# Linear attention and a gated feed-forward on one core: the order of batch 0's first steps, the pieces of w_out, and the last tile's banks

## The chip, the cores and the metric

The kernel runs on one core of one Trainium2 chip. The metric is the device time of an execution in microseconds (us). Before the change, four runs gave 313.59 to 313.95 us, with a median of 313.74 us.

A core has a matrix engine (TensorE, called PE in the profile), a vector engine (DVE), a scalar engine that evaluates functions (ACT), a general engine (POOL) and a synchronising engine (SP). Each has its own queue and runs it in order; they wait for one another through semaphores. POOL, SP and ACT also issue the transfers (DMAs) between main memory and on-chip memory. PE writes to PSUM, a small memory of eight banks of 512 float32 columns; DVE and ACT read results from there.

## The reference, cut to what matters

Eight batches of eight heads, 576 positions, head size 64. Linear attention comes first, then a gated feed-forward over all 4608 tokens of width 512 (inner width 1536):

```python
phi(x) = where(x > 0, x, exp(x) - 1) + 1
kv  = einsum('bhsd,bhse->bhde', phi(k), v)
z   = sum(phi(k), axis=positions)
num = einsum('bhsd,bhde->bhse', phi(q), kv)
den = einsum('bhsd,bhd->bhs', phi(q), z) + 1e-6
x   = (num / den), heads side by side          # 4608 x 512
g   = x @ w_gate
out = (silu(g) * (x @ w_val)) @ w_out
```

All inputs and the output are float32 in main memory; the kernel works in float16 with float32 sums.

## The kernel before, in words

**Tiling.** The 576 positions of a batch are cut into 9 slices (J) of 64. Two heads are stacked on the 128 partitions, so a tensor of one batch comes in two halves (lp = 0 and 1) of four heads each. The feed-forward works on groups of 512 tokens: eight units of 64 tokens each, nine groups in all. Group 0 is slices 0 to 7 of batch 0; group 1 takes slice 8 of batch 0 and slices 0 to 6 of batch 1. For a group, layer 1 has twelve steps (fb) of eight matmuls, 128x512 each, into a pair of PSUM banks; ACT takes the silu of the one bank, DVE multiplies by the other. Layer 2 has four tiles (t) of 128 tokens, with twelve matmuls each, whose result is copied to `osb` and stored in two DMAs.

**Order.** The order on each engine is the order in which the program's lines are written; nothing reorders it. PSUM is four pairs of banks (`pp4`), handed out in turn by `pair()`. Since phi(x) = max(x, 0) + min(exp(x), 1), phi of k is three steps: `exp_k` on ACT, `mx_k` and `mn_k` on DVE (and `add_k`, the sum of both).

**Batch 0's first steps** (the straight-line part from `nc.vector.tensor_copy(**q_cast(0))` on) are written by hand. q of batch 0 comes over SP. It is cast to float16, turned by PE into PSUM with 1 added (`q_one`, `q_turn`), two banks for each half: `qa` and `qb`. `q_exp` on ACT (L120) and `q_phi` on DVE (L454) make phi of q from each bank, four of each in all, written to `qT`. Meanwhile phi of k is made (L143, L147, L159). `zt` (L412) sums it over positions with small matmuls, and `zr_copy` (L416) brings the sums to `Zr`. `t_corners` (L254) multiplies `qT` by `Zr`, which gives the denominators. `lnrd` takes exp(-ln(den)) on ACT. `kv_corner` (L185) makes kv, `r_copy` (L201) brings it to `R`, `t_corners` with `R` gives the numerators, and `x_t` (L425) multiplies both into `xT`, the input of layer 1. `l1_mm` (L276) are the layer-1 matmuls of the first two steps, c being one of four slices of `xT`; later ones are at L292. `warm` issues matmuls (L124) whose result nobody reads.

The names X and Y are pairs made up of banks of `qb` and of another pair: Y's second bank is the one that holds the last quarter of turned q, so the second `t_corners(0, Zr, 1, Y)` can write it only when the last `q_phi` has read it.

**Loads.** POOL issues nearly all loads, in the written order; the program keeps eight of them on the way, so an issue waits until the one eight before it has landed. After the k and v of batch 0 and the layer-1 weights come, mixed: k of batch 1, w_out in pieces (`ld_w2`), q of batch 1 and its v. The twelve blocks of w_out are used by layer 2 of group 0 one after the other for all four tiles (L299). Inside that layer batch 1 is prepared: `s0` (after block 0) makes phi of q and k, `s1` (at block 6) turns q with 32 small matmuls (L374), `s2` (at block 7) sums z and turns slice 8, with copies at L381, L545 and L395, and after block 7 `s4` takes the denominators.

**The end.** The last tile of the last group is cut into columns 0 to 383 and 384 to 511 of one bank:

```python
for (n0, n1) in ((0, 384), (384, 512)):
    for fb in range(FB):
        l2_mm(g, t, fb, n0, n1)
    o = l2_out(g, t, "V" if n0 == 0 else "A", n0, n1, o)
```

`l2_out` copies with DVE ("V", L322) or ACT ("A", L120) and issues two stores (L326), on SP, but for the very last store, which ACT issues itself.

Of the kernel before, what the change touches and what calls it, by code (L numbers as in the profile page):

```python
# [17 lines left out]
def kernel(  # L18
# [10 lines left out]
    nc = tc.nc  # L29
# [9 lines left out]
    NG = B * J // U  # L39
# [22 lines left out]
    Zr = many([P, 2, 2, D], FP16, "Zr")  # L62
# [30 lines left out]
    def pair(p=None):  # L93
        i = 0 if p is None else [x is p for x in ring].index(True)
        p = ring.pop(i)
        ring.append(p)
        return p
# [4 lines left out]
    def ld(src, dst, b, lp):  # L102
        nc.gpsimd.dma_start(out=dst[b % NB][:, 2 * lp:2 * lp + 2, :],  # L103
                            in_=src[b].rearrange("(l a) (c j) d -> (a c) l (j d)", a=2, j=J)[:, 2 * lp:2 * lp + 2, :])
# [10 lines left out]
    def ld_w2(f0, f1):  # L115
        nc.gpsimd.dma_start(out=wo[:, f0:f1, :],
                            in_=moe_w_out[P * f0:P * f1, :].rearrange("(c p) f -> p c f", p=P))
# [4 lines left out]
    def warm(n, w=512, ps=None):  # L122
        for _ in range(n):
            nc.tensor.matmul(out=(ps or pp4[1][1])[:, 512 - w:512], lhsT=ones[:, :],  # L124
                             rhs=ones[:, 0:1].to_broadcast([P, w]), start=True, stop=True)
# [10 lines left out]
    def exp_k(b, lp):  # L136
        act(jl(ek, b, lp), lj(kr, b, lp), AF.Exp)
# [4 lines left out]
    def mx_k(b, lp):  # L142
        nc.vector.tensor_scalar(out=jl(kp, b, lp), in0=lj(kr, b, lp), scalar1=0.0, scalar2=None, op0=ALU.max)  # L143
# [35 lines left out]
    def kv_corner(b, lp, t, first, last):  # L179
        ps = kvp[b]  # L180
        for j in range(J):
            for l2 in range(2):
                for hh in range(2):
                    rows = slice(C * hh, C * hh + C)
                    nc.tensor.matmul(out=ps[hh][D * l2:D * l2 + D, D * lp:D * lp + D],  # L185
                                     lhsT=t[b % 2][rows, lp, j, D * l2:D * l2 + D],
                                     rhs=vr[b % NB][rows, 2 * lp + l2, D * j:D * j + D],
                                     start=(first and j == 0), stop=(last and j == J - 1))
# [107 lines left out]
    l2p = {}  # L296
# [17 lines left out]
    def l2_out(g, t, eng, n0=0, n1=512, o=None):  # L314
        if o is None:
            o = osb[on[0] % 4]
            on[0] += 1
        ps = l2p[(g, t)]
        if eng == "A":
            act(o[:, n0:n1], ps[:, n0:n1], scale=1.0 / SC)  # L320
        else:
            nc.vector.tensor_scalar(out=o[:, n0:n1], in0=ps[:, n0:n1], scalar1=1.0 / SC, scalar2=None, op0=ALU.mult)  # L322
        for e in range(2):
            b, j = units(g)[0][2 * t + e]
            dma = nc.scalar if g == NG - 1 and t == 3 and n1 == 512 and e == 1 else nc.sync
            dma.dma_start(out=out[S * b:S * b + S, n0:n1].rearrange("(c j) f -> j c f", j=J)[j],  # L326
                              in_=o[C * e:C * e + C, n0:n1])
        return o
# [17 lines left out]
    ld(k, kr, 1, 1)  # L346
    ld_w2(0, 4)
    ld(q, qr, 1, 0)
    ld(q, qr, 1, 1)
    ld_w2(4, 6)  # L350
    ld_w2(6, 8)
    ld_w2(8, 12)
    ld2(v, vr, 1)
# [56 lines left out]
    def zt(b, lp, ps, t, first, last):  # L410
        for j in range(J):
            nc.tensor.matmul(out=ps[:, 0:2], lhsT=t[b % 2][:, lp, j, :], rhs=ob[:, 0:P:C],  # L412
                             start=(first and j == 0), stop=(last and j == J - 1))

    def zr_copy(b, lp, ps):
        nc.vector.tensor_scalar(out=Zr[b][:, lp, :, :], in0=ps[:, 0:2].unsqueeze(2).to_broadcast([P, 2, D]),  # L416
                                scalar1=1.0 / SC, scalar2=None, op0=ALU.mult)

    def lnrd(ps, i, w0=0, w1=512):
        for l2 in range(2):  # L420
            act(lnt[2 * i + l2][:, w0:w1], ps[l2][:, w0:w1], AF.Ln, bias=epsb[:, 0:1])
            act(rd[i][:, l2, w0:w1], lnt[2 * i + l2][:, w0:w1], AF.Exp, scale=-1.0)
# [4 lines left out]
    def x_t(g, lp, ps, l2s=(0, 1)):  # L427
        for l2 in l2s:
            xmul(xT[g % 2][:, 2 * lp + l2, :], ps[l2][:, :], rd[lp][:, l2, :])

    def t_corners(g, W, lp, ps):
        for (b, j0, j1, c0) in units(g)[1]:
            corners(ps, W[b], b, lp, j0, j1, c0)
# [15 lines left out]
    def q_exp(lp, h, pair_):  # L449
        act(q_half(lp, h), pair_[h][:, :], AF.Exp, bias=m1[:, 0:1])  # L450

    def q_phi(lp, h, pair_):
        a = q_half(lp, h)
        nc.vector.scalar_tensor_tensor(out=a, in0=pair_[h][:, :], scalar=1.0, in1=a, op0=ALU.max, op1=ALU.min)  # L454

    kvp[0] = pp4[1]
    X = [pp4[0][0], pp4[3][0]]
# [17 lines left out]
    warm(WARM[1])  # L475
    q_turn(1, qb)
    q_exp(1, 0, qb)
    q_exp(1, 1, qb)
    exp_k(0, 0)
    warm(WARM[2])  # L480
    exp_k(0, 1)
    q_phi(0, 0, qa)
    q_phi(0, 1, qa)
    q_phi(1, 0, qb)
    mx_k(0, 0)
    q_phi(1, 1, qb)
    mn_k(0, 0)
    mx_k(0, 1)
    zt(0, 0, X[1], kp, True, False)
# [9 lines left out]
    kv_corner(0, 0, kp, True, True)  # L499
    r_copy(0, 0, 1, "VV")  # L500
    zt(0, 1, Y[0], ek, False, True)
    warm(WARM[5], ps=X[0])
    zr_copy(0, 1, Y[0])
    t_corners(0, R, 0, X)
    x_t(0, 0, X, (0,))
    kv_corner(0, 1, kp, True, False)
    kv_corner(0, 1, ek, False, True)
    r_copy(0, 1, 2, "VV")
    t_corners(0, Zr, 1, Y)
    lnrd(Y, 1)  # L510
    x_t(0, 0, X, (1,))
    l1_mm(0, 0, pp4[2], (0,))
    l1_mm(0, 1, X, (0,))
    t_corners(0, R, 1, pp4[1])
# [153 lines left out]
    for g in range(NG):  # L668
        b1, b2 = g + 1, g + 2
        if g == 0:  # L670
            sl = period0()
        else:
            sl, _ = none()
            late = []
            if g == 1:
                sl[1] = [lam(zsum, b1)]
                sl[4] = [lam(phi_q, b1, 0)]
                sl[5] = [lam(phi_q, b1, 1), lam(zb, b1)]
                ch = chain(b1, 6)
                late = ch.pop(10) + ch.pop(11)  # L680
            elif b1 < B:
                sl[0] = [lam(phi_q, b1, 0)]
                sl[1] = [lam(phi_q, b1, 1)]
                ch = chain(b1, 2)
            else:
                ch = {}
            for f, v_ in ch.items():
                sl[min(f, FB - 1)] += v_
        for fb in range(FB):
            if g == 0:  # L690
                if fb < 2:
                    continue
                if fb == 4:
                    ld2(k, kr, 2)
                    ld2(q, qr, 2)
                    ld2(v, vr, 2)
            if g == 1 and fb < 2:
                if fb == 0:
                    two = [pair(), pair()]
                    for cs in ((0, 1), (2, 3)):  # L700
                        for i in range(2):
                            l1_mm(g, i, two[i], cs)
                l1_post(g, fb, two[fb])
            else:
                l1(g, fb)
            for f in sl[fb]:
                f()
        if g + 3 < B:
            if g > 0:
                nc.gpsimd.tensor_copy(out=gate[:, :], in_=qT[b1 % 2][:, 1, J - 1, 1, C - 1:C])  # L710
            ld2(k, kr, g + 3)
            ld2(v, vr, g + 3)
            if g > 0:
                ld2(q, qr, g + 3)
        if g == 0:
            layer2_0()
            ld2(q, qr, 3)
        else:
            for f in late:
                f()  # L720
            for t in range(4):
                if t == 0 and b2 < B:
                    if g == 1:
                        nc.scalar.preload_act_table_set("natural_log_exp_and_others")
                    exp_k(b2, 0)
                    exp_k(b2, 1)
                    exp_q(b2, 0)
                    exp_q(b2, 1)
                    phi_k(b2, 0)
                    phi_k(b2, 1)  # L730
                    zsum(b2)
                if t == 1 and g == 1:
                    kv_all(b1)
                    r_copy(b1, 0, 2, "AA")
                if t == 3:
                    block(g)
                if g == NG - 1 and t == 3:
                    l2_open(g, t)
                    o = None
                    for (n0, n1) in ((0, 384), (384, 512)):  # L740
                        for fb in range(FB):
                            l2_mm(g, t, fb, n0, n1)
                        o = l2_out(g, t, "V" if n0 == 0 else "A", n0, n1, o)
                    continue
                lay2(g, t)
                l2_out(g, t, "A" if g == 1 and t == 1 else "AV"[t % 2])
            if b2 < B:
                zb(b2)
# [30 lines left out]
```

## Time and profile before

| What | Value |
|---|---|
| median of four runs | 313.74 us |
| the profiled execution's own time | 313.46 us |
| its span, first to last instruction | 311.7 us |
| PE busy | 304.8 us (98%) |
| DVE busy | 205.1 us (66%) |
| ACT busy | 152.6 us (49%) |
| layer-1 matmuls (L292) | 57.6% of the chain that ended last |
| layer-2 matmuls (L299) | 30.4% of that chain |
| read from main memory | 37.75 MB |

The profile is one execution. Its times count from the first instruction, and the time around the span (1.76 us here) is start and end of the execution. A row of the timeline gives start and length in us, engine, line and operation, what is written from what, the shape, how many, and in brackets the engine's idle time before it and what ended that. "The chain that ended last" is followed back from the last instruction, at each step to what released it. A transfer is shown with its issue; its landing is the issue plus the time to landing.

### The profile page before, as it was taken

Reading aid. Unit: us, or ns where it says so; the run is one execution under the profiler, and the core shown is the slowest. Engines: PE = TensorE matmul, PEld = TensorE weight load, DVE = VectorE, ACT = ScalarE, POOL = GpSimd, SP = SyncE. Lnnn points to the kernel's source line nnn. Section 1 sums busy time; section 2 is a strip of 40 time slices with the busy share of each in tenths; the row PEclk is TensorE's granted clock in tenths of the full one; section 3 lists DMA queues with packets and bytes.
Section 4 is the critical chain, followed back from the end, with each engine's and each line's share of the span. In section 5 each row is a group of like instructions: output and inputs, shape, how many; then the busy total and the mean of one; then the engine's idle time right before and its main releaser. Section 6 shows DMA issues by size and latency. Waiting matters only on the chain.

```text
span 311.7 us, 5565 instructions
## 1 busy us (share of the span) xinstructions
PE 304.8 (98%) x2206; PEld 141.7 (45%) x2206; DVE 205.1 (66%) x361; ACT 152.6 (49%) x231; POOL 48.5 (16%) x73
## 2 busy tenths in 40 slices
PE   7999999999999999999999999999999999999994
PEld 3444454444544454445444544454444444444442
DVE  4755868999699658976697759874981434143410
ACT  4865959448733844374536643574330333133311
POOL 8745444400000410041000500000000000000000
PEclk9999999999999999999999999999999999999999
DMA  8999999998502693239612990323032300140014
GB/s 218 198 197 200 206 207 236 234 207 147 118 13 39 98 196 110 40 57 184 162 38 41 130 235 12 64 52 87 0 75 53 85 1 1 43 93 0 2 34 101
DMA packets 41178, 32.80 MB, mean 105 GB/s; under 512 B 16448, under 2 KB 36160, under 8 KB 41152
## 3 DMA queue, kind: packets, MB, share of 16 engines
q0 software_dynamic: 20480, 18.29, 37.5%
q1 hardware_dynamic: 20592, 14.13, 18.9%
q8 instruction: 17, 0.28, 0.3%
q14 instruction: 9, 0.07, 0.1%
q10 hardware_dynamic: 80, 0.03, 0.0%
HBM read 37.75 MB, written 9.44 MB: 151 GB/s over the span
## 4 chain that ended last, share of the span: by engine, by line
PE 95%; DVE 2%; DMA 1%; SPq 0%; issue 0%; ACT 0%; DVEq 0%
PE pp L292 58%; PE pp L299 30%; PE pp L276 2%; PE pp L254 2%; PE pp L185 2%; DMA q<-in_q_dram 1%; DVE qT L454 1%; PE pp L124 1%; DVE xT L425 0%; PE pp L412 0%; PE pp L212 0%; PE pp L374 0%; DVE osb L322 0%; SPq L333 0%; DVE qp L467 0%
## 5 line engine op out<-in xcount | busy, mean ns | idle before, releaser
L120 ACT ACTIVATE sil<-pp 128x512 f16<-128x512 f32 x108 | 63.4, 597 | 101.0 <-PE pp L292 97.5
L292 PE MATMUL pp<-xT,wg 128*128 128x512 f16 x416 | 106.8, 379 | 0.0
L292 PE MATMUL pp<-xT,wv 128*128 128x512 f16 x416 | 106.8, 379 | 0.0
L285 DVE SCALAR_TENSOR_TENSOR hT<-pp,sil 128x512 f16<-128x512 f32 x108 | 72.3, 681 | 47.9 <-PE pp L292 35.3
L299 PE MATMUL pp<-wo,hT 128*128 128x512 f16 (+2 forms) x444 | 97.1, 373 | 0.6 <-DVE osb L322 0.6
L299 PEld LDWEIGHTS <-hT 128*128 128x128 f16 x444 | 41.9, 98 | 49.9 <-issue 2.1
L292 PEld LDWEIGHTS <-wv 128*128 128x128 f16 x416 | 40.7, 98 | 49.1
L292 PEld LDWEIGHTS <-wg 128*128 128x128 f16 x416 | 40.7, 98 | 48.4
L322 DVE TENSOR_SCALAR osb<-pp 128x512 f32<-128x512 f32 (+1 forms) x19 | 12.9, 682 | 31.1 <-PE pp L299 26.7
L120 ACT ACTIVATE osb<-pp 128x512 f32<-128x512 f32 (+1 forms) x18 | 10.3, 574 | 34.8 <-PE pp L299 34.8
L120 ACT ACT_TABLE_LOAD x13 | 16.7, 1283 | 2.5 <-PE pp L292 2.4
L120 ACT ACTIVATE ek<-kr 128x1152 f16<-128x1152 f16 x16 | 17.8, 1157 | 0.1
L229 DVE TENSOR_TENSOR qp<-qp,rden 128x1152 f16<-128x1152 f16 x12 | 16.2, 1346 | 0.0
L220 DVE TENSOR_REDUCE den<-prod 128x18 f32<-128x1152 f16 x12 | 16.1, 1344 | 0.0
L710 POOL COPY gate<-qT 128x1 f16<-128x1 f16 x4 | 1.1, 277 | 96.3 <-DMA qT<-qp 96.3
L120 ACT ACTIVATE eq<-qr 128x1152 f16<-128x1152 f16 x14 | 15.4, 1151 | 0.0
L103 POOL DMA_DIRECT2D vr<-in_v_dram x16 | 11.9, 744 | 8.5 <-DMA wo<-in_moe_w_out_dram 2.4
L271 DVE TENSOR_SCALAR xT<-pp 128x512 f16<-128x512 f32 (+1 forms) x14 | 8.8, 667 | 6.5 <-PE pp L254 6.5
L103 POOL DMA_DIRECT2D kr<-in_k_dram x16 | 11.6, 728 | 8.6 <-DMA wo<-in_moe_w_out_dram 1.9
L159 DVE TENSOR_TENSOR kp<-ek,kp 128x1152 f16<-128x1152 f16 x15 | 11.4, 758 | 0.5
L147 DVE TENSOR_SCALAR ek<-ek 128x1152 f16<-128x1152 f16 x16 | 7.8, 490 | 5.0 <-ACT ek L120 5.0
L103 POOL DMA_DIRECT2D qr<-in_q_dram x14 | 10.2, 729 | 5.3 <-DMA qr<-in_q_dram 2.3
(86 smaller groups left out, 179.5 us busy)
## 6 DMA issues: line engine op xcount, KB each, us to landing
out_dram<-osb SPq DMA_DIRECT2D x70, 128.0 KB, 2.8
kr<-in_k_dram POOLq DMA_DIRECT2D x16, 288.0 KB, 8.6
vr<-in_v_dram POOLq DMA_DIRECT2D x16, 288.0 KB, 10.1
qr<-in_q_dram POOLq DMA_DIRECT2D x14, 288.0 KB, 11.8
wg<-in_moe_w_gate_dram POOLq DMA_DIRECT2D x5, 256.0 KB, 9.4
wv<-in_moe_w_val_dram POOLq DMA_DIRECT2D x5, 256.0 KB, 10.3
q<-in_q_dram SPq DMA_DIRECT2D x2, 576.0 KB, 4.1
wo<-in_moe_w_out_dram POOLq DMA_DIRECT2D x2, 512.0 KB, 12.4
```

The costliest lines, as they stand in the source:

```text
L103: nc.gpsimd.dma_start(out=dst[b % NB][:, 2 * lp:2 * lp + 2, :], in_=src[b].rearrange("(l a) (c j) d -> (a c) l (j d)", a=2, j=J)[:, 2 * lp ...
L120: nc.scalar.activation(out=out, in_=in_, func=func, bias=bias, scale=scale)
L147: nc.vector.tensor_scalar(out=a, in0=a, scalar1=1.0, scalar2=None, op0=ALU.min)
L159: nc.vector.tensor_tensor(out=a, in0=ek[b % 2][:, lp, :, :], in1=a, op=ALU.add)
L185: nc.tensor.matmul(out=ps[hh][D * l2:D * l2 + D, D * lp:D * lp + D], lhsT=t[b % 2][rows, lp, j, D * l2:D * l2 + D], rhs=vr[b % NB][rows, 2 ...
L220: nc.vector.tensor_reduce(out=den[:, c, :], in_=prod[:, :, :].rearrange("p j (l d) -> p (j l) d", d=D), axis=AX.X, op=ALU.add)
L229: nc.vector.tensor_tensor(out=qv, in0=qv, in1=rden[:, c, :].unsqueeze(2).to_broadcast([P, 2 * J, D]), op=ALU.mult)
L271: nc.vector.tensor_scalar(out=dst, in0=ps[l2][:, c0:], scalar1=1.0 / SC, scalar2=None, op0=ALU.mult)
L285: nc.vector.scalar_tensor_tensor(out=hT[g % 2][:, fb, :], in0=ps[1][:, :], scalar=SC, in1=s[:, :], op0=ALU.mult, op1=ALU.mult)
L292: nc.tensor.matmul(out=ps[h][:, :], lhsT=w[:, c, P * fb:P * fb + P], rhs=xT[g % 2][:, c, :], start=(c == 0), stop=(c == 3))
L299: nc.tensor.matmul(out=l2p[(g, t)][:, n0:n1], lhsT=hT[g % 2][:, fb, P * t:P * t + P], rhs=wo[:, fb, n0:n1], start=(fb == 0), stop=(fb == F ...
L322: nc.vector.tensor_scalar(out=o[:, n0:n1], in0=ps[:, n0:n1], scalar1=1.0 / SC, scalar2=None, op0=ALU.mult)
```

## The change

There are four edits. In batch 0's first steps, ACT's first exp of k now stands ahead of q's last exp, DVE's first max of k ahead of q's third phi, and q's last phi behind the second z copy; the second denominators are taken before the second half of the kv matmuls of `ek`, and both first x products are issued together. One block of w_out is loaded between the two halves of batch 1's q, and the next one right behind them, in place of one piece of two blocks. The last tile is cut at column 320, its first part is copied by ACT and its second by DVE, the second part goes to the first bank of the next pair, and of each part's two stores ACT issues the second.

```diff
-            dma = nc.scalar if g == NG - 1 and t == 3 and n1 == 512 and e == 1 else nc.sync
+            dma = nc.scalar if g == NG - 1 and t == 3 and e == 1 else nc.sync
...
     ld(q, qr, 1, 0)
+    ld_w2(4, 5)
     ld(q, qr, 1, 1)
-    ld_w2(4, 6)
+    ld_w2(5, 6)
     ld_w2(6, 8)
...
     q_exp(1, 0, qb)
+    exp_k(0, 0)
     q_exp(1, 1, qb)
-    exp_k(0, 0)
     warm(WARM[2])
     exp_k(0, 1)
     q_phi(0, 0, qa)
     q_phi(0, 1, qa)
+    mx_k(0, 0)
     q_phi(1, 0, qb)
-    mx_k(0, 0)
-    q_phi(1, 1, qb)
     mn_k(0, 0)
     mx_k(0, 1)
...
     zt(0, 1, Y[0], ek, False, True)
+    zr_copy(0, 1, Y[0])
+    q_phi(1, 1, qb)
     warm(WARM[5], ps=X[0])
-    zr_copy(0, 1, Y[0])
     t_corners(0, R, 0, X)
-    x_t(0, 0, X, (0,))
+    x_t(0, 0, X)
     kv_corner(0, 1, kp, True, False)
+    t_corners(0, Zr, 1, Y)
+    lnrd(Y, 1)
     kv_corner(0, 1, ek, False, True)
     r_copy(0, 1, 2, "VV")
-    t_corners(0, Zr, 1, Y)
-    lnrd(Y, 1)
-    x_t(0, 0, X, (1,))
     l1_mm(0, 0, pp4[2], (0,))
...
-                    for (n0, n1) in ((0, 384), (384, 512)):
+                    for (n0, n1) in ((0, 320), (320, 512)):
                         for fb in range(FB):
                             l2_mm(g, t, fb, n0, n1)
-                        o = l2_out(g, t, "V" if n0 == 0 else "A", n0, n1, o)
+                        o = l2_out(g, t, "A" if n0 == 0 else "V", n0, n1, o)
+                        l2p[(g, t)] = pair()[0]
```

## The prediction

> **What bounds the kernel now.** I read the page first (TensorE, PE, is busy 98% of the span), then the chain of work that ended last in order of time, then the timeline of single engines where that chain leaves PE. The chain, as start and length in us:
>
> ```profile
> 8.64 0.38 DVE kp L143
> ...
> 9.06 0.39 PE pp L412 x9
> ...
> 14.76 0.38 PE pp L276
> 15.13 0.34 PE pp L254 x4
> 15.47 2.78 PE pp L276 x12
> 18.25 17.27 PE pp L292 x80
> ...
> 306.90 0.57 DVE osb L322
> ...
> 307.51 0.84 PE pp L299 x12
> ...
> 308.38 0.28 ACT osb L120
> ```
>
> From about 15.4 to 306.9 us PE is fed without a hole; that stretch is a fixed amount of matmul work that the change doesn't touch. So only three places can move the end: the head up to 15.4, the tail after 306.9, and a place in between where a transfer or the vector engine (DVE) is only just in time and a PE that comes earlier would have to wait. The head, by engine (start, length, what ended the idle time before it):
>
> ```profile
> 7.23 1.27 ACT L120 ACTIVATE qT<-pp,m 128x512 f16<-128x512 f32 x2 [0.41 <-PE pp L442]
> 8.38 1.16 ACT L120 ACTIVATE ek<-kr 128x1152 f16<-128x1152 f16 x1
> 8.55 0.45 DVE L143 TENSOR_SCALAR kp<-kr 128x1152 f16<-128x1152 f16 x1
> 8.92 0.68 DVE L454 SCALAR_TENSOR_TENSOR qT<-pp,qT 128x512 f16<-128x512 f32 x1
> 9.58 0.46 DVE L147 TENSOR_SCALAR ek<-ek 128x1152 f16<-128x1152 f16 x1
> 11.39 0.69 ACT L120 ACTIVATE lnt<-pp,epsb 128x512 f32<-128x512 f32 x1 [0.79 <-PE pp L254]
> ```
>
> The max of k (8.55) stands behind three phi steps of q, and ACT's first exp of k (8.38) behind four of q. The place in between is layer 2 of the first group, where batch 1's q arrives. POOL's queue tells the landings: each issue waits for the DMA eight issues before it, and its row names it.
>
> ```profile
> 34.47 0.71 POOL L103 DMA_DIRECT2D kr<-in_k_dram  x1 [1.90 <-DMA wo<-in_moe_w_out_dram]
> 35.88 0.80 POOL L103 DMA_DIRECT2D kr<-in_k_dram  x1 [0.70 <-DMA qr<-in_q_dram]
> 37.27 0.75 POOL L103 DMA_DIRECT2D qr<-in_q_dram  x1 [0.58 <-DMA qr<-in_q_dram]
> 38.55 0.71 POOL L103 DMA_DIRECT2D qr<-in_q_dram  x1 [0.53 <-DMA wo<-in_moe_w_out_dram]
> ```
>
> So w_out's first piece, q's two halves and w_out 4 to 6 are seen about 1.3 to 1.4 us apart. The second half of q was issued at 25.08 and took 11.9 us, so it landed at 36.98, and the vector engine picks it up a little later:
>
> ```profile
> 37.05 0.82 DVE L384 TENSOR_SCALAR qp<-qr 128x1152 f16<-128x1152 f16 x2
> 37.80 0.48 DVE L155 TENSOR_SCALAR eq<-eq 128x1152 f16<-128x1152 f16 x1
> ...
> 42.74 0.42 DVE L545 TENSOR_SCALAR Zr<-pp 128x256 f16<-128x256 f32 x1 [0.48 <-PE pp L543]
> 43.09 0.48 DVE L395 COPY qT<-pp 128x256 f16<-128x256 f16 x2
> ```
>
> PE's next num/den matmuls start at 43.62, right after the second copy ends (43.57). DVE works almost without a hole from 37.05; its only slack is the 0.48 us before 42.74.
>
> **Head: phi and exp moved.** No instruction is added or removed. ACT's first exp of k moves in front of q's last exp: from 8.38 to about 7.82 (7.23 plus half of the pair, 0.59); the k half has landed by then (POOL's issue at 7.59 was released by it). It ends at 8.98. On DVE the max of k takes the place of the third phi (7.95 instead of 8.55, ends 8.38 instead of 9.01), that phi follows, and the min can start at 9.01, when exp ends, instead of 9.58. On PE the two z sums with four warm-up matmuls between (0.86) start when the max ends: 8.43 instead of 9.06, and the second comes 0.63 earlier too, since the min (ends 9.47) and the warm-ups (end 9.52) are both done. From there the chain is z copy, denominator matmuls, and then eight ACT steps (ln, exp of the reciprocal) back to back from 11.39 to 16.45; all shift by 0.63. The last x product (16.49) and with it the last four layer-1 matmuls of the first pair shift likewise, and layer 1 starts at 17.46 instead of 18.09.
>
> What the moved work costs: q's last phi (0.68) now runs at about 12.02 to 12.70, behind the z copy. Waiting for it are the second denominator matmuls (13.41 before; now 12.75 at the soonest) and, queued behind it on DVE, the first x product: 13.10 before, now 12.63, only 0.47 earlier. Neither decides: ACT takes the second denominators only at 13.26, and the second x product waits for ACT's reciprocal at 13.33, 0.65 earlier than before. The kv copies of the second half now stand behind both x products, near 14.0 to 14.3 instead of 13.71 to 14.05, but the numerator matmuls that read them waited for the fourth layer-1 matmul (14.76), which waited for that x product; they still go out at 14.4 instead of 15.06. Sum of the head: PE is 0.63 earlier at layer 1. The weights allow it: w_val's second block is needed at 18.32 and lands at 18.0.
>
> **w_out in pieces around q.** The second half of q gets one 128 KB piece of w_out ahead of it. The pieces of 256 KB and the halves of 288 KB land 1.3 and 1.4 us apart, so 128 KB is 0.64. By the Trainium skill (DMA: Bandwidth & Descriptors, "Anatomy of one DMA — SWDGE (gpsimd) path") a DMA on this path costs about 2.0 us plus its bytes at 436 GB/s, which is 2.3 us for 128 KB. The first weight pieces speak for the smaller figure:
>
> ```profile
> wg<-in_moe_w_gate_dram POOLq DMA_DIRECT2D x2, 128.0 KB, 8.0
> wv<-in_moe_w_val_dram POOLq DMA_DIRECT2D x2, 128.0 KB, 7.9
> ```
>
> Issued at 4.30, 5.01, 5.72 and 6.48, they landed 8.0, 8.0, 7.9 and 7.9 us later, so 0.7 apart: in a full queue the fixed part overlaps. I take 0.64, with 0.5 and 2.3 as ends. POOL issues one DMA more (0.71), hidden in a queue that runs 11 to 12 us ahead of the landings; later loads carry the same bytes and land when they did.
>
> So q's second half lands at 37.62. DVE's second max of q starts at 37.64; queued behind it are all of q's and k's phi steps, the copies of the transposes and the two copies that release PE. Their chain in the trace, from the second max (37.42) to the end of the last copy (43.57), is 6.15 less the 0.48 of idle: 5.67. (The min at 37.80 waited for ACT's exp; that comes earlier now.) Start 37.64 gives 43.31, PE at 43.36 instead of 43.62. PE arrives at the transposes at 40.0 and waits about 0.6 there. Of the 0.63 that the head gains, 0.25 is left. The other w_out blocks come in time: block 4 is needed at 38.2 and is there at 36.3, block 5 at 39.0 and 38.3. Without this edit PE would wait about 0.15 for block 4 and q would be on time, so this edit by itself costs some 0.25.
>
> After 43.4 everything is 0.25 earlier. The next transfer with little slack is batch 1's v: its last half was issued at 31.86 and took 13.1, so it landed at 44.95, and is needed at 46.1 with the lead. The lead reaches the tail.
>
> **Tail.** Before, the last 128 columns wait until DVE has copied the first 384, because both are in one bank (PE's idle 0.65 is put down to "DVE osb L322"). Now the second part has a bank of its own that was last read in layer 1. PE runs all 12 x 512 columns without a hole: an ordinary tile takes 2.59, the tile before ended at 304.91, so PE is done at 307.50 instead of 308.35: 0.85. The last copy is 128x192 on DVE: from 0.56 for 384 and 0.69 for 512 columns, 0.36; the head's 128x128 at 0.29 says the same. It was 0.28 on ACT: minus 0.08. Handing over between engines, where ACT triggered its own DMA, minus 0.03. The last stores are 48 KB, between 32 KB (1.9 to 2.0) and 96 KB (2.1): minus 0.02. ACT's copy of 320 columns (0.44, between 0.28 and 0.60) and its first issue (0.56) end by 307.6, before the second issue at 307.9; SP likewise. Sum 0.72.
>
> **Sum.** 0.25 + 0.72 = 0.97 off the profiled execution's 313.46 (span 311.7, and 1.76 around it that nothing here touches): 312.5. That execution is 0.28 under the median of 313.74, so the median comes to 312.8.
>
> **Rivals.** (a) The lead of the head survives whole, if the piece delays q less or the chain behind it has more slack than I see: 0.63 + 0.72, 312.4. For it: DVE's short steps here take 0.45 to 0.64 for one size, so the chain has some give. Against it: the rows place q's landing only 0.44 before its use at 37.42, less than the piece's 0.64.
> (b) The lead is lost whole: q comes 0.9 or more later, or DVE's k phi steps are slowed by POOL's descriptor writing as at 40.23 (0.64, against 0.46 at 9.58). Only the tail is left: 313.0.
> (c) The tail doesn't pay: the second bank waits for something, or the stores end as late as before. Then 0.25 is left: 313.5.
> (d) Slower: the piece in front of q costs the page's 2.3. PE starts at 42.72 plus the piece, so above 0.90 the head loses, above 1.62 it eats the tail's gain and above 2.25 the kernel is slower by 0.2%. At 2.3 it is 1.40 lost and 0.72 gained: 314.4.
>
> **How the numbers follow.** Likeliest 0.57, (a) 0.16, (b) 0.13, (c) 0.08, (d) 0.06. A measurement of this kernel can tell about 0.2% (0.63 us) from no change. Likeliest and (a) lie beyond it, and (b) partly (0.03): faster 0.76; same 0.18 with (c) and most of (b); slower 0.06. The range from 312.3 to 313.3 holds the likeliest, (a) and (b).
>
> **What would show it.** Right: max of k near 7.9, the ln steps near 10.8, layer 1 at 17.5; a hole on PE before the transposes near 40.3, the denominators at 43.4; no hole between the last two parts and a last copy ending near 307.65 (307.90 less the 0.25). Wrong: a wait for q's second half well past 37.7, a wait for weights in layer 1 before 18.3, or a PE hole before the last 192 columns.

## The result, and the profile after

The changed kernel takes 312.78 us (median of 29 runs, 312.36 to 314.11); the kernel before, beside it, 313.60 (47 runs, 313.43 to 314.51). The ratio is 0.9974, with a 95% interval of 0.9969 to 0.9979: 0.26% less, or 0.82 us. The forecast was 312.8. The profiled execution took 312.39 (span 310.6), near the lowest of its runs, against 313.46 (span 311.7) before: 1.07 less. That the median shows less than the two profiles is something the forecast has no word for.

The chain of the work that ended last, of the changed kernel, through the head (start and length in us, what):

```profile
7.92 1.06 ACT ek L120
...
9.00 0.46 DVE ek L147
9.46 0.64 DVE kp L143
...
10.96 0.62 DVE ek L147
...
11.63 0.40 PE pp L413 x9
...
12.06 0.29 DVE Zr L417
12.35 0.61 DVE qT L455
...
13.00 0.40 PE pp L254 x2
...
13.74 0.97 PE pp L276 x4
14.71 0.34 PE pp L254 x4
15.05 2.78 PE pp L276 x12
17.83 17.27 PE pp L292 x80
```

The last row but one started at 15.47 before, and layer 1's steady run (last row) at 18.25: the head brought 0.42 us. Q's moved phi (12.35) stands on this chain, where the forecast had put it beside the chain. In the timeline layer 1's first matmul starts at 17.66 instead of 18.09, so I call the lead 0.43.

The second place, where batch 1's q arrives, on DVE (timeline of the changed kernel; the brackets say what ended the idle time):

```profile
36.63 0.45 DVE L385 TENSOR_SCALAR qp<-qr 128x1152 f16<-128x1152 f16 x1
37.58 0.46 DVE L385 TENSOR_SCALAR qp<-qr 128x1152 f16<-128x1152 f16 x1 [0.50 <-DMA qr<-in_q_dram]
37.96 0.45 DVE L155 TENSOR_SCALAR eq<-eq 128x1152 f16<-128x1152 f16 x1
...
42.32 0.42 DVE L545 TENSOR_SCALAR Zr<-pp 128x256 f16<-128x256 f32 x1
42.66 0.48 DVE L396 COPY qT<-pp 128x256 f16<-128x256 f16 x2
```

The two maxima that were one run at 37.05 are apart: the second waits 0.50 us for q's second half. The 0.48 us of idle before the copy to `Zr` is gone. The copies end at 43.14, and PE takes the denominators at 43.19 instead of 43.62: all of the 0.43 is still there.

The end (chain of the changed kernel):

```profile
296.72 10.40 PE pp L299 x60
307.12 0.02 issue
307.15 0.36 DVE osb L322
```

PE's last 60 matmuls are one piece; before, 48 and 12 with 0.65 between. The last copy ends at 307.51 instead of 308.66.

### The profile page after: what moved, and what is told of

Its sections match the earlier page's. It is cut to its first block, busy times and chain, and to the rows that moved or that the text cites. A ratio compares the mean times of both kernels' runs of the same rounds, so it can differ in the third digit from the quotient of the medians.

```text
span 310.6 us, 5568 instructions
## 1 busy us (share of the span) xinstructions
PE 304.4 (98%) x2206; PEld 141.9 (46%) x2206; DVE 204.7 (66%) x361; ACT 153.0 (49%) x231; POOL 48.8 (16%) x74
## 4 chain that ended last, share of the span: by engine, by line
PE 95%; DVE 1%; DMA 1%; ACT 1%; SPq 0%; issue 0%
PE pp L292 58%; PE pp L299 30%; PE pp L276 2%; PE pp L254 2%; PE pp L185 2%; DMA q<-in_q_dram 1%; DVE ek L147 0%; ACT ek L120 0%; ACT qT L120 0%; DVE kp L159 0%; PE pp L212 0%; DVE kp L143 0%; DVE qT L455 0%; PE pp L375 0%; DVE Zr L417 0%; SPq L333 0%
```

## The experiments

The first four kernels take the change apart. All four ran on one chip, beside the same runs of the kernel before (median 313.67).

**The tail alone.** The edit is the last part of the change's diff and its first line, on the kernel before.

```diff
-                    for (n0, n1) in ((0, 384), (384, 512)):
+                    for (n0, n1) in ((0, 320), (320, 512)):
...
-                        o = l2_out(g, t, "V" if n0 == 0 else "A", n0, n1, o)
+                        o = l2_out(g, t, "A" if n0 == 0 else "V", n0, n1, o)
+                        l2p[(g, t)] = pair()[0]
```

> The kernel before with the tail's edits alone (cut at 320, a bank of its own for the second part, ACT then DVE, ACT issues two stores). The forecast's sum: 0.72 us less than before. Read from the changed kernel's trace, where the last store took 2.12 us and not 2.0: 0.62 less. Rival (the tail doesn't pay): no change. PE without a hole ahead of the last 192 columns in all cases but the rival.

Measured: 313.03 us (11 runs, 312.73 to 313.25), ratio 0.9976 [0.9962, 0.9989], 0.64 less. This is most of the whole gain, and its runs lie within 0.5 us.

**The order of the first steps alone.** The diff's part from `q_exp(1, 0, qb)` to `l1_mm(0, 0, pp4[2], (0,))`.

> The kernel before with the order of batch 0's first steps alone. The forecast's lead is 0.63 us at layer 1, less about 0.15 of waiting for block 4 of w_out: 0.45 to 0.5 less than before. From the changed kernel's trace the lead is 0.43 only, since two of DVE's short steps take 0.25 longer, and block 4 is then just in time: 0.4 less. Rival (the lead is lost at the next transfer): under 0.1 less.

Measured: 313.43 us, but from 313.07 to 314.25 (11 runs), ratio 1.0001 [0.9991, 1.0010]. No sure gain: six runs lie 0.2 to 0.6 under the median of before, five at it or above. The profiled run (313.74) shows what the upper ones can look like (timeline of the order alone):

```profile
7.58 0.67 DVE L454 SCALAR_TENSOR_TENSOR qT<-pp,qT 128x512 f16<-128x512 f32 x1
...
8.71 1.16 ACT L120 ACTIVATE ek<-kr 128x1152 f16<-128x1152 f16 x1 [0.47 <-DMA kr<-in_k_dram]
8.71 0.46 DVE L143 TENSOR_SCALAR kp<-kr 128x1152 f16<-128x1152 f16 x1 [0.45 <-DMA kr<-in_k_dram]
```

K of batch 0 landed at 8.69, and both engines waited for it, 0.45 to 0.47 us; in the profile of before it had landed at 7.30. The old order wants k at 8.38, the new one at 7.82. Batch 0's q was late too: it landed at 6.19, in the profile of before at 5.89, and put these steps back by 0.3 us before k did. Layer 1 started at 18.34, later than the 18.09 of before.

**The pieces of w_out alone.**

```diff
+    ld_w2(4, 5)
     ld(q, qr, 1, 1)
-    ld_w2(4, 6)
+    ld_w2(5, 6)
```

> The kernel before with the pieces of w_out around q alone. q's second half lands 0.64 us later. The forecast's chain on DVE has 0.48 of idle to take that up, and q waited 0.44 before: no change in time, within 0.1. If a piece costs the page's 2.3 us: 1.4 slower.

Measured: 313.74 us (313.49 to 313.96), ratio 1.0003 [0.9994, 1.0012]: no difference. Q's second half landed 1.43 us after the piece, and the piece 0.61 after q's first half, so a piece in a full queue costs its bytes. The rival with 2.3 us is out. This trace also shows the old order with a late q of batch 0: it landed at 6.24, 0.35 later than in the profile of before, k (7.65) was in time, the max of k began at 8.89 and layer 1 at 18.43, both 0.34 later. So in the old order a late q went into the start of layer 1 in full.

**Order and tail, without the pieces.**

> The changed kernel without the pieces of w_out: order and tail alone. The forecast said that the pieces cost 0.25 us, so this one is 0.25 faster than the changed kernel, 1.2 less than before. The rival reading of the changed trace, in which PE had no wait for q at all at the transposes: the pieces cost nothing, and this is within 0.1 of the changed kernel, or slower by the wait for block 4 of w_out.

Measured: 312.72 us (312.30 to 313.45), ratio 0.9963 [0.9940, 0.9987]. The changed kernel has 312.78, so the pieces cost nothing that can be seen in the medians; these intervals are too wide to rule out 0.25, and the traces have to decide. In this one PE starts layer 2 at 34.86, reaches block 4 at 38.48 instead of 38.31 (16 matmuls of 0.216 us), because that block lands at 38.44, and takes the denominators at 43.29. Without the pieces PE waits 0.17 for w_out. With them q comes later, but in the first profile of the changed kernel the denominators followed layer 2's start by the same 8.26 us as before: nothing was lost. So the forecast's 0.25 for the pieces is wrong for these traces.

Beside the tail alone (313.03, on the same chip) this kernel shows what the order adds: 0.31 off the median, and nine of its eleven runs lie under 313.03. The intervals of the two ratios overlap, so the size of this is not sure.

**Q later still.** If q's landing is the next bound, a larger piece ahead of it must show at once.

```diff
-    ld_w2(4, 5)
+    ld_w2(4, 6)
     ld(q, qr, 1, 1)
-    ld_w2(5, 6)
```

> The changed kernel with blocks 4 and 5 of w_out in one piece ahead of the second half of batch 1's q, which so lands another 0.64 us later. If q's landing and DVE's chain behind it are the next bound, as the forecast has it, the denominators start 5.6 us after q lands: 0.65 us slower than the changed kernel, about 0.2 less than before. If that chain still has slack, no slower than the changed kernel.

Measured: 313.49 us (312.90 to 314.19, 10 runs), ratio 0.9995 [0.9986, 1.0003]: 0.7 slower than the changed kernel, as the bound has it. (The changed kernel's 312.78 was not taken beside this run; the kernel before has 313.58 beside this one and 313.60 beside that.) PE in that trace (timeline):

```profile
40.13 0.41 PE L374 MATMUL pp<-id,qp 64*128 64x64 f16 x16
41.01 0.41 PE L374 MATMUL pp<-id,qp 64*128 64x64 f16 x16 [0.48 <-DVE qp L387]
...
43.77 0.64 PE L254 MATMUL pp<-qT,Zr 64*64 64x64 f16 x16
```

The transposes are cut in two: the second half waits 0.48 us for DVE's sum of the second half of q. The wait that I had forecast for the changed kernel is here. Five traces side by side:

| Trace | q's second half lands | layer 2 starts | denominators start | after q | after layer 2's start |
|---|---|---|---|---|---|
| before | 36.98 | 35.36 | 43.62 | 6.64 | 8.26 |
| order and tail | 37.17 | 34.86 | 43.29 | 6.12 | 8.43 |
| changed | 37.56 | 34.93 | 43.19 | 5.63 | 8.26 |
| q later still | 38.15 | 34.85 | 43.77 | 5.62 | 8.92 |
| changed, second profile | 38.37 | 35.24 | 43.98 | 5.61 | 8.74 |

The denominators start 8.26 us after layer 2 begins or 5.62 after q lands, whichever is later; order and tail adds its 0.17 of waiting for block 4. With that, all thirteen traces fit to about 0.01. In the first profile of the changed kernel both are met at once, to within 0.01.

**One bank.** The tail's edits without the second bank.

```diff
-                        l2p[(g, t)] = pair()[0]
```

> The tail's edits alone, but both parts in one bank. If the second bank is what pays, PE waits for ACT's copy of 320 columns (0.44) and there is no gain: within 0.1 of before. If the other cut, the other engines and ACT's second store pay, most of the 0.64 of the tail stays.

Measured: 313.79 us (313.55 to 314.55), ratio 1.0005 [0.9996, 1.0015]. The whole gain of the tail hangs on this line (timeline of the kernel with one bank):

```profile
306.70 0.44 ACT L120 ACTIVATE osb<-pp 128x320 f32<-128x320 f32 x1 [1.03 <-PE pp L299]
...
307.19 1.15 PE L299 MATMUL pp<-wo,hT 128*128 128x192 f16 x12 [0.53 <-ACT osb L120]
...
308.44 0.36 DVE L322 TENSOR_SCALAR osb<-pp 128x192 f32<-128x192 f32 x1 [5.26 <-PE pp L299]
```

PE waits 0.53 us for ACT's copy. The other cut, the other engines and ACT's second store bring nothing without the second bank. The second bank with the old cut was not run.

**K later.** Whether k's landing bounds the new order, tried the other way: the first half of v goes ahead of k.

```diff
-    ld2(k, kr, 0)
-    ld2(v, vr, 0)
+    ld(v, vr, 0, 0)
+    ld2(k, kr, 0)
+    ld(v, vr, 0, 1)
```

> The changed kernel with the first half of batch 0's v loaded ahead of k, so that k lands 1.4 us later, near 8.8 to 9.5. If k's landing bounds the new order (in the trace of the order alone it landed at 8.69 and the max started at 8.71), the max of k waits for it and the head is 0.9 to 1.4 us later: 0.1 to 0.6 slower than before in spite of the tail. If k's landing doesn't bound it, as the forecast took it, no slower than the changed kernel.

Measured: 313.91 us (313.10 to 316.14, 10 runs), ratio 1.0010 [0.9993, 1.0027]: 1.1 slower than the changed kernel. K landed at 9.05 (timeline):

```profile
9.07 0.46 DVE L143 TENSOR_SCALAR kp<-kr 128x1152 f16<-128x1152 f16 x1 [1.16 <-DMA kr<-in_k_dram]
```

Against the changed kernel's profile the max of k starts 1.22 later, and layer 1 and the denominators 1.04 later. So a late k goes into the time nearly one to one. Where k is first and all of q comes over SP, nine traces put its landing at 7.20, 7.30, 7.39, 7.65, 7.91, 7.94, 8.02, 8.04 and 8.69. One of nine is past the 8.38 that the old order wants, five past the 7.82 of the new one, four of these by 0.22 at most.

**The changed kernel again**, with its own trace:

> The changed kernel itself, beside the next two on one chip: 0.8 us less than before as on record, with a spread of over 1 us.

Measured: 312.69 us (5 runs, 312.49 to 313.21; before 313.65 on this chip), ratio 0.9966 [0.9954, 0.9979]. The profiled run is the slowest of the five, and shows where else the lead goes (timeline of PE):

```profile
17.55 1.03 PE L292 MATMUL pp<-xT,wg 128*128 128x512 f16 x4
18.83 1.04 PE L292 MATMUL pp<-xT,wv 128*128 128x512 f16 x4 [0.25 <-DMA wv<-in_moe_w_val_dram]
```

Here the head's lead was 0.54. W_val's second block landed at 18.78 and not at 18.0, so PE waited for it (four matmuls take 0.86, the next four came 1.28 later), and q landed 0.8 later than in the first profile (last row of the table).

**Two tries to bring k sooner failed.** First, slice 8 of batch 0's q, needed only in layer 1, was loaded later on POOL's queue:

```diff
-        nc.sync.dma_start(out=q32[:, h:h + 2, :],
-                          in_=q[0].rearrange("(l a) (c j) d -> (a c) l (j d)", a=2, j=J)[:, h:h + 2, :])
+        nc.sync.dma_start(out=q32[:, h:h + 2, 0:8 * D],
+                          in_=q[0].rearrange("(l a) (c j) d -> (a c) l (j d)", a=2, j=J)[:, h:h + 2, 0:8 * D])
...
     ld_w1(512, 768)
+    nc.gpsimd.dma_start(out=q32[:, :, 8 * D:9 * D],
+                        in_=q[0].rearrange("(l a) (c j) d -> (a c) l (j d)", a=2, j=J)[:, :, 8 * D:9 * D])
```

> The changed kernel with slice 8 of batch 0's q, which is needed only in layer 1, loaded later on POOL's queue: 128 KB less ahead of k. q lands 0.3 and k 0.6 us earlier, so that k is there before the max wants it. If the landings at the start bound the head, it is 0.3 to 0.6 faster than the changed kernel, 1.1 to 1.4 less than before, with a smaller spread. If not, as fast as the changed kernel.

Measured: 313.13 us (312.74 to 314.13), ratio 0.9984 [0.9975, 0.9993]: by the medians 0.35 slower than the changed kernel, though the two intervals just touch; faster it is not. Q landed sooner (5.53), but in the profiled run, the slowest of twelve, k landed at 8.83. Second, the second half of q went to the head of POOL's queue:

```diff
-    for h in (0, 2):
-        nc.sync.dma_start(out=q32[:, h:h + 2, :],
+    for (h, dma) in ((0, nc.sync), (2, nc.gpsimd)):
+        dma.dma_start(out=q32[:, h:h + 2, :],
```

> The changed kernel with the second half of batch 0's q loaded at the head of POOL's queue and not on SP's, so that k follows q in one queue. In the traces so far k landed 1.3 to 3.3 us after q, which came over another queue, and 7.2 to 8.8 us from the start. If the late landings come from the two queues taking turns, k lands at 7.3 to 7.5 each time, the max of k starts at 7.9, and the time is that of the changed kernel's best executions: 1.0 to 1.1 less than before, with a spread of about 0.5. If k lands as late as before or q later than 5.9, no gain over the changed kernel.

> The order of batch 0's first steps alone, with the same load of q. Alone, without that load, the order gave no sure gain (ratio 1.000). If k's late landing had eaten it, 0.4 us less than before here. If the order has no gain of its own, none.

Measured: 314.73 us (ratio 1.0034 [1.0016, 1.0052]) and 316.79 us (1.0093 [1.0079, 1.0107]). This q landed at 7.50 and 7.33 instead of 5.9 and k behind it at 8.95 and 9.38, so neither run says anything on the order with an early k: the load that was moved came later itself. Why k's landing spreads is open: the next loads follow it at fixed steps of about 1.43 us, so it is the beginning of POOL's transfers that moves, but no run moved it on purpose without moving something else.

## Why the prediction was right, step by step

**Head, 0.63 forecast, 0.43 measured in the profile.** The first steps came as worked out: max at 7.85 (forecast 7.9), min at 9.00, second z sum at 9.52, ln at 10.80 (10.8). Then two durations failed. I took DVE's second max and second min of k as 0.45 us from the trace of before; they took 0.73 and 0.69 (timeline of the changed kernel):

```profile
9.11 0.74 POOL L112 DMA_DIRECT2D wv<-in_moe_w_val_dram  x1 [0.51 <-DMA kr<-in_k_dram]
9.38 0.73 DVE L143 TENSOR_SCALAR kp<-kr 128x1152 f16<-128x1152 f16 x1
...
10.58 0.74 POOL L112 DMA_DIRECT2D wg<-in_moe_w_gate_dram  x1 [0.73 <-DMA vr<-in_v_dram]
...
10.89 0.69 DVE L147 TENSOR_SCALAR ek<-ek 128x1152 f16<-128x1152 f16 x1
```

Both began inside an issue of POOL and ended 0.26 us after it. POOL's issues are tied to landings and hardly moved (9.01 and 10.49 before); DVE's steps moved under them. The long min held up the z sums, these the moved phi, that the second denominators, at 13.00 and not 12.75, and ACT took up its third ln at 13.44 instead of 13.26. So "Neither decides" was wrong: second denominators that come 0.25 late make the ln 0.18 late, so they had only 0.07 us to spare. Where the two steps were not stretched and k came at 7.94 or 7.91, the lead at layer 1 was 0.50 and 0.54. There ACT's first exp of k began when k was there, at 7.96 and 7.93 and not at 7.82; with that 0.14 and 0.11 the forecast's 0.63 is back. The chain was right, and two of its inputs, the length of DVE's steps and k's landing, were not. The old order meets POOL's issues too: in the traces of the tail alone and of one bank the second min took 0.72 us, and layer 1 began at 18.30 and 18.27; with the late q of the pieces alone it began at 18.43. The 18.09 that the lead is counted from is the earliest of these four.

**Pieces.** The piece's 0.64 was right (q at 37.56, forecast 37.62), and so was the chain behind q, to 0.11: from landing to denominators 5.63 against 5.74. That the edit costs 0.25 was wrong. It rested on a lead of 0.63; with 0.43 q's chain ends just when PE gets there anyway (with 0.5 some 0.07 would be lost), and without the pieces PE waits 0.17 for block 4. The forecast left 0.25 of the head; the profile kept 0.43. A lead that was sized too high and a loss that followed from it cancelled in part.

**Tail, 0.72 forecast, 0.62 in the profile, 0.64 in the median.** From the start of the last layer 2 to the end of the last copy the tail became 0.73 shorter (forecast 0.74). The last store took 2.12 us and not 2.02. But its size isn't the reason: in three other traces with the old tail ACT's last store, of 32 KB, took 2.12 to 2.13 as well. It was the trace of before that had a quick one, 2.03, and the forecast was built on it.

**Sum.** 0.97 forecast, 1.07 between the two profiles, 0.82 between the medians. That the forecast's 312.8 is met to 0.02 is luck: it took 313.74 from four runs as the median of before, where 47 runs give 313.60, and the gain is 0.15 smaller than forecast; the two errors cancel. That the medians show less than the profiles goes with the spread of the landings. The kernel before could wait for k until 8.38 and for q with 0.44 to spare; its runs lie close together. The new order has used these margins up, and an execution in which k, w_val or either q lands late gives part of the lead back. The runs with k and q later show the price, nearly one to one; how many ordinary runs pay it is argued from nine traces, not counted.

**Rivals.** (a), the lead survives, was right in the first profile's place (nothing was lost at q) and wrong on its size. (b), the lead is lost, is what single executions do, by late loads; its second reason, DVE's steps slowed beside POOL's issues, took 0.2 of the lead in the head. (c) is refuted by the tail alone, (d) by the pieces alone.

## What to carry to other kernels

When an engine is to start earlier, look for what it will then arrive at: here every 0.1 us beyond 0.43 would have met a landing, so the steady part of the gain was the bank at the end, and the order added about 0.3 us in most runs and nothing in others. A margin against a transfer is judged by the spread of its landing over several traces, not by the one at hand. Durations of a short step hold only for the place where it was measured: a step that moves may run beside another engine's work that it did not meet before.

## What the runs showed of the hardware

**DVE behind POOL's issues.** In all thirteen traces' first 60 us, 172 of DVE's 214 max and min steps of 128x1152 float16 last 0.44 to 0.46 us. The other 42 are just those that began 0.21 to 0.48 us before the end of one of POOL's DMA issues (about 0.74 long): all of them ended 0.26 us after that issue's end (one 0.28), and so lasted up to 0.74. The 39 that began earlier in an issue, 0.59 us or more before its end, were not stretched. The Trainium skill (SBUF — State Buffer, "Who interferes with whom") has such a step of DVE and an instruction of POOL shut each other out for the whole instruction. The stretching fits that in part; but here the two ran side by side through most of an issue, and only DVE steps paid that, at their usual 0.45 us, would still have been running 0.03 us before its end.

**PE's clock after a short hole.** In the trace of the order alone with q on POOL, PE stood idle for 2.01 us before q's second half (timeline, and then stretches with the granted clock as the first number after POOL's count):

```profile
8.18 0.62 PE L442 MATMUL pp<-id,qp 128*128 128x128 f16 x8 [2.01 <-DVE qp L468]
8.63 2.29 PE L124 MATMUL pp<-ones 128*128 128x512 f16 x5
```

```profile
6.00:9.00 3.00, 0.99 (x10) 0.57 (x10) 1.65 (x4) 1.20 (x3) 2.13 (x3) 0.94 1.14 198
9.00:12.00 3.00, 3.00 (x17) 1.28 (x16) 2.20 (x5) 2.89 (x4) 1.50 (x2) 0.50 1.21 203
```

The clock was 0.50 from 9 to 12, and five 512-column matmuls took 2.29 us instead of 1.25. In its sister with the whole change the hole was 1.84 us long and the clock stayed at 1.00. So a part of this kernel's 3 us of loss is the clock's, and not the order's; how large a part was not measured. These are two traces, and that the length of the hole decides is not shown.
